# Threshold attention and a SoLU feed-forward: in batch 0, turned weights that stay in place but for corner blocks, and 1/sum multiplied in behind v

## The chip, the cores and the metric

The kernel runs on one core of a Trainium2 chip. Its time is the device time of one launch, in microseconds (us). A profile is one further execution recorded by the hardware profiler. The core has five engines that run their own instruction lists in order and wait for one another by semaphores: TensorE (PE; its weight loads are listed as PEld), VectorE (DVE), ScalarE (ACT), GpSimd (POOL) and SyncE (SP), which here only issues DMAs.

## What is computed

All data are float32 but for the two weight matrices, which are given as float64.

```python
# q, k, v: (8 batches, 8 heads, 576, 64); tau: a number
scores = q @ k.T / sqrt(64)
scores = where(scores >= max(scores, -1) - tau, scores, -1e9)
attn = exp(scores - max(scores, -1))
attn = attn / (sum(attn, -1) + 1e-9)
x = heads_side_by_side(attn @ v)                 # (4608, 512)
h = x @ w_in                                     # (4608, 1024)
solu = h * softmax(h)
ln = (solu - mean) / sqrt(var + 1e-6) * g_ln
out = ln @ w_out                                 # (4608, 512)
```

## The kernel before

**Slots and rounds.** A slot is the scores of 128 query rows against 576 keys for two heads. A batch has 18 slots (`PER`): for each kind (0 and 1) and each of four head pairs two slots (r = 0 and 1), and two slots of kind 2 for the last 64 query rows of all heads. Two slots that follow one another (r = 0, 1) are a unit: they are multiplied with v together. The main loop (line 855) goes through 144 slots and some rounds more; round `rnd` does the scores of slot `rnd`, the second half of slot `rnd - 1`, the product with v of an older unit, and a quarter of a feed-forward tile. Everything lies under `tc.manual_schedule()`: each engine executes its instructions in the order in which the loop writes them.

**One slot.** TensorE writes the scores of both heads to PSUM (`scores`, L434). VectorE goes over them twice, once a head (`maxes`, L455), for row minimum (the scores have a negative sign) and threshold. ScalarE makes the ramp (`ramp`, L470) and the exponentials with their row sums (`exps`, L479) into the tiles `w`. One round later GpSimd makes 1/(sum + 1e-9) (`normalise`, L486 and L487) and multiplies both `w` by it (L489). VectorE then turns `w` in blocks of 32 x 32 (`blocks`, L501) into the tile `T`. When the second slot of a unit is turned, SP's queue moves the whole of `T` to the tile `wT` (L510, L512, for kind 2 L517), which brings the keys onto the partitions of v: one transfer of 576 KB and two of 288 KB, or four of 288 KB. Some rounds later (`pv_due`, line 751: three rounds behind the second slot, four for some) TensorE multiplies v by `wT` in 72 matmuls a unit (`attend_steps`, L542) into a PSUM room, and ScalarE copies that room to the feed-forward's input (`attended`, L572).

**PSUM rooms.** Two rooms `p0` and `p1` serve the product with v, the feed-forward, and in rounds 0, 2 and 4 the turning of q and k of batch 0 (`whole_pair`, L371), which ScalarE copies to SBUF (`keep`, L388 and L390).

**Order inside a round.** In program order: `scores`, `maxes`, `ramp`, `exps`; `whole_pair` in three early rounds; `normalise` of the slot before; jobs of the list `middle` (the feed-forward's statistics, L650); `weight_c`; the feed-forward's step on TensorE (L605 or L710) and the product with v; `attended`; `blocks` of the slot before; jobs of the list `late` (the feed-forward's maximum L620, its multiply L635, its turn L697); and then the weights.

**Weights.** Both weight matrices come as float64 and are put together as float32 from their two 32-bit words, sixteen pieces of 128 x 512, about one a round in rounds 0 to 14. `weight_load` (L251) brings a piece, ScalarE prepares the low word (`weight_e`, L263), VectorE scales the high word by 2^-112 (`weight_m`, L282), masks and shifts it (L286) and sets the sign (`weight_b`, L308), and GpSimd adds the low part one round later (`weight_c`, L332). For the second matrix ScalarE multiplies the gains in (`weight_f`, L340).

**Feed-forward tiles.** The first tile of 128 tokens starts in round 11 (L605, two rounds a tile), its second product (L710) in rounds 17 and 18.

## Time and profile before

| | us |
|---|---|
| runs of the kernel | 857.89, 856.11, 856.63; median 856.63 |
| span of the profiled execution | 854.9 |
| median above that span | 1.7 |

The time of the profiled execution itself isn't listed apart from its span. In rows of groups the columns are line, engine, operation, what is written from what, shapes and count, then busy us, mean ns of one, and the idle time of the engine before them with what ended it. In rows in order of time they are start us, length us, engine, line, operation, and in brackets idle time with its releaser; "x2" is two instructions put together. In rows by stretch they are the stretch, its length, busy us and number of instructions of TensorE, its weight loads, VectorE, ScalarE and GpSimd, then TensorE's granted clock, the DMA share and GB/s. TensorE's busy time counts matmuls that overlap one another, so it isn't a measure of its peak.

### The profile page before, as it was taken

To read this page: it belongs to the slowest core of one execution; us is meant where nothing else is said; L and a number is where in the kernel's file an instruction comes from. 1 tells how busy PE (TensorE), PEld (TensorE's weight loads), DVE (VectorE), ACT (ScalarE), POOL (GpSimd) and SP (SyncE) were. 2 spreads that over 40 slices of the span, in tenths; PEclk is the share of its full clock that TensorE was granted. 3 is DMA by queue.
4 is the path that set the end of the run, shared out by engine and by line. 5 is a ranking of instruction groups with operands and counts; after the bars stand their busy time and mean duration, and the time that the engine had idled before them with its cause. 6 is when DMAs were issued, how large, how long until landed. Compare 5 with 4: busy or idle time off the path is not lost.

```text
span 854.9 us, 36109 instructions
## 1 busy us (share of the span) xinstructions
PE 819.9 (96%) x15363; PEld 620.5 (73%) x15363; DVE 674.6 (79%) x1225; ACT 570.0 (67%) x1127; POOL 496.1 (58%) x945
## 2 busy tenths in 40 slices
PE   6778899999999999999999999999999999999997
PEld 5555677778677787777688877777777777777655
DVE  5997787989788888888788878888888878787361
ACT  6886876777767666667666666666677777775121
POOL 4885656666566656565566666565666655555120
PEclk8899999999999999999999999999999999999999
DMA  9999778798888888887888778887788887655212
GB/s 343 254 249 213 191 194 233 188 259 204 226 229 202 211 185 218 216 216 190 201 215 218 195 177 209 207 217 207 195 221 226 207 188 175 165 137 140 67 38 63
DMA packets 75314, 168.54 MB, mean 197 GB/s; under 512 B 11146, under 2 KB 32658, under 8 KB 75154
## 3 DMA queue, kind: packets, MB, share of 16 engines
q1 hardware_dynamic: 74866, 165.82, 76.7%
q8 instruction: 120, 1.97, 1.0%
q10 hardware_dynamic: 288, 0.43, 0.2%
q14 instruction: 40, 0.33, 0.1%
HBM read 46.14 MB, written 9.44 MB: 65 GB/s over the span
## 4 chain that ended last, share of the span: by engine, by line
PE 83%; DMA 4%; DVE 4%; ACT 3%; issue 2%; POOL 2%; SPq 1%; DVEq 0%; ACTq 0%; POOLq 0%
PE o_ps L710 27%; PE h_ps L605 22%; PE s_ps L434 15%; PE pv L542 14%; DMA wT<-T 3%; PE h_ps L595 3%; ACT w L470 1%; DVE w L455 1%; ACT w L479 1%; DVE T L501 1%; POOL w L489 1%; POOL sm L487 0%; PE s_ps L379 0%; DVE w L308 0%; PE tp L371 0%
## 5 line engine op out<-in xcount | busy, mean ns | idle before, releaser
L710 PE MATMUL o_ps<-w,uT 64*64 64x256 f32 x4608 | 269.5, 376 | 2.2 <-issue 1.6
L470 ACT ACTIVATE w<-s_ps,nth 128x576 f32<-128x576 f32 x280 | 196.8, 738 | 105.6 <-DVE nth L455 88.6
L455 DVE CUSTOM_DVE_ANT_0 w<-s_ps,tau_t 128x576 f32<-128x576 f32 x280 | 200.0, 751 | 83.5 <-PE s_ps L434 52.4
L710 PEld LDWEIGHTS o_ps<-w,uT 64*64 64x64 f32 x4608 | 221.8, 133 | 55.4 <-ACT xh L572 12.0
L489 POOL TENSOR_SCALAR w<-w,sm 128x576 f32<-128x576 f32 x288 | 220.6, 778 | 14.3
L501 DVE STREAM_TRANSPOSE T<-w 128x576 f32<-128x576 f32 x288 | 207.7, 756 | 22.6 <-POOL w L489 22.3
L605 PE MATMUL h_ps<-w,xh 64*64 64x512 f32 x1856 | 220.8, 589 | 0.0
L479 ACT ACTIVATE w<-w,ntau 128x576 f32<-128x576 f32 x288 | 219.6, 767 | 0.0
L542 PEld LDWEIGHTS pv<-wT,v 64*64 64x64 f32 x5760 | 172.6, 136 | 39.8 <-issue 16.7
L434 PE MATMUL s_ps<-kT,qT 64*64 64x512 f32 (+1 forms) x2048 | 175.8, 416 | 13.4 <-ACT w L470 11.3
L542 PE MATMUL pv<-wT,v 64*64 64x128 f32 (+1 forms) x5760 | 173.9, 263 | 8.3 <-DMA wT<-T 7.4
L605 PEld LDWEIGHTS h_ps<-w,xh 64*64 64x64 f32 x1856 | 118.4, 133 | 77.2 <-issue 43.6
L486 POOL TENSOR_SCALAR sm<-sm 128x2 f32<-128x2 f32 x144 | 34.2, 237 | 186.5 <-ACT w L479 182.8
L487 POOL TENSOR_TENSOR sm<-sm,mone 128x2 f32<-128x2 f32 x144 | 106.7, 741 | 12.0
L434 PEld LDWEIGHTS s_ps<-kT,qT 64*64 64x64 f32 x2048 | 72.7, 137 | 21.7 <-ACT w L470 16.2
L572 ACT COPY xh<-pv 128x256 f32<-128x256 f32 x64 | 25.4, 396 | 80.9 <-PE pv L542 80.9
L671 ACT ACTIVATE V<-u,nb,rs 128x1024 f32<-128x1024 f32 x36 | 44.7, 1240 | 40.5 <-POOL nb L661 33.6
L697 DVE STREAM_TRANSPOSE uT<-V 128x1024 f32<-128x1024 f32 x36 | 44.1, 1225 | 15.9 <-DMA V<-u 15.6
L479 ACT ACTIVATION_READ_ACCUMULATOR w<-w,ntau 128x1 f32 x288 | 55.4, 192 | 0.0
L676 DVE TENSOR_SCALAR u<-u,rs,nb 128x1024 f32<-128x1024 f32 x36 | 34.9, 971 | 19.5 <-ACT V L671 17.9
L635 DVE TENSOR_TENSOR u<-h_ps,u 128x1024 f32<-128x1024 f32 x36 | 42.8, 1190 | 9.4 <-ACT u L629 9.4
L620 DVE TENSOR_REDUCE hm<-h_ps 128x1 f32<-128x1024 f32 x36 | 42.9, 1193 | 4.9 <-PE h_ps L595 2.7
(77 smaller groups left out, 553.5 us busy)
## 6 DMA issues: line engine op xcount, KB each, us to landing
wT<-T SPq DMA_DIRECT2D x160, 288.0 KB, 6.5
wT<-T SPq DMA_DIRECT2D x64, 576.0 KB, 5.5
v<-in_v_dram SPq DMA_DIRECT2D x16, 576.0 KB, 6.0
V<-u SPq DMA_DIRECT2D x144, 64.0 KB, 3.5
out_dram<-ob SPq DMA_DIRECT2D x71, 128.0 KB, 2.6
q<-in_q_dram SPq DMA_DIRECT2D x28, 288.0 KB, 6.1
k<-in_k_dram SPq DMA_DIRECT2D x27, 288.0 KB, 6.4
qT<-flip SPq DMA_DIRECT2D x48, 144.0 KB, 3.2
```

What stands on the lines that cost most here:

```text
L434: nc.tensor.matmul(out=ps[h][ROWS[y], ks], lhsT=lhsT, rhs=d["kT"][ROWS[h], ks], start=True, stop=True,)
L455: nc.vector.tensor_tensor_reduce(out=w, in0=ps[:, 0:S], in1=(zero if loose else tau_t).to_broadcast([P, S]), scale=1.0, scalar=BIG, op0=AL ...
L470: nc.scalar.activation(out=d["w"][x], in_=d["w"][x] if d["loose"] else d["ps"][x][:, 0:S], func=AF.Prelu, bias=d["nth"][x], scale=-1.0, al ...
L479: nc.scalar.activation(out=w, in_=w, func=AF.Exp, bias=ntau, scale=1.0, accum_out=sm[:, x : x + 1])
L487: nc.gpsimd.tensor_tensor(out=sm, in0=sm, in1=mone, op=ALU.pow)
L489: nc.gpsimd.tensor_scalar(out=w, in0=w, scalar1=sm[:, x : x + 1], scalar2=1.0, op0=ALU.mult, op1=ALU.mult)
L501: nc.vector.transpose(out=T[:, :, r, h, :], in_=w)
L542: nc.tensor.matmul(out=to, lhsT=d["v"][ROWS[u], (h0 + h - u) % 4, m,], rhs=rhs, start=m == 0, stop=m == NK - 1,)
L605: mm = nc.tensor.matmul(out=h[ROWS[y], f], lhsT=x[ROWS[r], c, ROWS[y]], rhs=w1_parts[ROWS[r], c, part ^ r], start=part == 0 and c == 0, st ...
L671: nc.scalar.activation(out=V, in_=u, func=AF.Identity, bias=nb, scale=rs)
L697: nc.vector.transpose(out=uT, in_=d["V"].rearrange("p y (m x) -> p m y x", x=32))
L710: nc.tensor.matmul(out=d["o"][ROWS[z], 512 * (r ^ other) : 512 * (r ^ other) + 256], lhsT=d["uT"][ROWS[r], m].rearrange("p y x -> p (y x)" ...
```

## The change

It concerns batch 0 alone (slots 0 to 17), but for the shared helper functions.

- `keep` stores the turned k of batch 0 without reordering its columns, so that keys come in chunks of 64.
- `normalise` makes 1/sum as before and no longer multiplies `w`. The sums live in six buffers.
- `corners` takes the place of `blocks`. VectorE turns `w` into `T`, now in an order in which half of the blocks already lie on the partitions where the product needs them. GpSimd copies each turned slot to a second tile `more`; after the second slot four DMAs bring the corner blocks from `more` back into `T` (4 x 32 partitions, 147 KB each). The product reads `T` itself. `corners` returns the copy as a function, which the loop calls behind `weight_b`.
- `spread` is new: behind the product, eight small matmuls by the identity write 1/sum into the same PSUM room, and ScalarE copies it to SBUF. In `attended` two VectorE multiplies take the place of ScalarE's copy for batch 0.
- `weight_s` is new: GpSimd does the scaling by 2^-112 for pieces 4 to 10, two rounds ahead; `weight_m` skips L282 for these.
- `pv_due`: units of slots 1, 3, 5 and 11 come one round earlier.
- `ff_o`: the two output halves of batch 0 are no longer swapped for the second tile.

```diff
@@ weight_m
+            of = d.get("scaled", m)
+            if of is m:
+                nc.vector.tensor_scalar(
+                    out=m.bitcast(F32), in0=hi.bitcast(F32), scalar1=2.0**-112, scalar2=None,
+                    op0=ALU.mult,
+                )
             nc.vector.tensor_scalar(
-                out=m.bitcast(F32), in0=hi.bitcast(F32), scalar1=2.0**-112, scalar2=None,
-                op0=ALU.mult,
-            )
-            nc.vector.tensor_scalar(
-                out=m, in0=m, scalar1=0x7FFFFFFF, scalar2=3,
+                out=m, in0=of, scalar1=0x7FFFFFFF, scalar2=3,
...
+    def weight_s(x):
+        if in_bits(x):
+            hi = raws[x]["raw"].bitcast(F32).rearrange("p (n two) -> p n two", two=2)[:, :, 1]
+            dst = piece(x)[1]
+            nc.gpsimd.tensor_scalar(
+                out=dst, in0=hi, scalar1=2.0**-112, scalar2=1.0, op0=ALU.mult, op1=ALU.mult
+            )
+            raws[x]["scaled"] = dst.bitcast(I32)
@@ keep
         if nm == "k":
+            if i < NP:
+                of, to = room[:, 0 : 64 * len(ms)], pair(i)["kT"][:, 64 * ms[0] : 64 * ms[-1] + 64]
@@ exps
-        d["sm"] = sm = small.tile([P, 2], F32, tag="sm", name="sm")
+        d["sm"] = sm = small.tile(
+            [P, 2], F32, tag="late" if s < PER else "sm", bufs=6 if s < PER else 3, name="sm"
+        )
@@ normalise
         nc.gpsimd.tensor_tensor(out=sm, in0=sm, in1=mone, op=ALU.pow)
+        if s < PER:
+            return
...
+    def corners(s):
+        b, kind, hp, r = slots[s]
+        key = (b, kind, hp)
+        if r == 0:
+            units[key] = dict(
+                T=work.tile([P, NB, 2, 2, 32], F32, tag="T", name="T"),
+                more=work.tile([P, NB, 2, 2, 32], F32, tag="wT", bufs=2, name="wT"),
+                rc=[],
+            )
+        u = units[key]
+        d = live.pop(s)
+        u["rc"].append(d["sm"])
+        T, more = [u[x].rearrange("p (c m) r h x -> p c m r h x", c=2) for x in ("T", "more")]
+        for h, w in enumerate(d["w"]):
+            nc.vector.transpose(out=T[:, :, :, r, h], in_=w.rearrange("p (m c x) -> p c m x", m=NK, c=2))
+
+        def copy():
+            of, to = [u[x][:, :, r].rearrange("p k h x -> p k (h x)") for x in ("T", "more")]
+            nc.gpsimd.tensor_copy(out=to, in_=of)
+            if r == 0:
+                return
+            of, to = [x.rearrange("p c m r h x -> p c (m r h x)") for x in (more, T)]
+            for g in range(2):
+                for half in range(2):
+                    at, src = 64 * half + 32 * (1 - g), 64 * half + 32 * g
+                    nc.sync.dma_start(out=to[at : at + 32, g], in_=of[src : src + 32, 1 - g])
+            u["wT"] = T.rearrange("p g m r h x -> p g m r h x")
+
+        return copy
...
+    def spread(key):
+        b, kind, hp = key
+        unit = units[key]
+        y = unit["y"][1].rearrange("p (u n) -> p u n", u=2)[:, :, 256:384]
+        for r, rc in enumerate(unit["rc"]):
+            for u in range(2):
+                for h in range(2):
...
+                    nc.tensor.matmul(
+                        out=to, lhsT=rc[ROWS[u], h : h + 1].to_broadcast([64, 64]),
+                        rhs=ident[ROWS[u], ROWS[u]].rearrange("p (g x) -> p g x", g=2), start=True, stop=True,
+                    )
+        unit["by"] = by = unit["more"].rearrange("p k r h x -> p (k r h x)")[:, 0:256].rearrange(
+            "p (u n) -> p u n", u=2
+        )
+        nc.scalar.copy(out=by, in_=y)
@@ attended
+        if b == 0:
+            spread(key)
+            by = units[key]["by"]
...
-        nc.scalar.copy(out=to, in_=y)
+        if b == 0:
+            for u in range(2):
+                nc.vector.tensor_tensor(out=to[:, u], in0=y[:, u], in1=view(by)[:, u], op=ALU.mult)
+        else:
+            nc.scalar.copy(out=to, in_=y)
@@ ff_o
-        other = len(t) == 3 and t[2]
+        other = len(t) == 3 and t[0] > 0 and t[2]
@@ the plan
+    LATE = (PER - 1, PER + 9)
+    SCALED = range(4, 11)
...
-            pv_due.append((s + LAG_PV + (s < 6 or s in (11, PER - 1, PER + 9)), (b, kind, hp)))
+            pv_due.append((s + LAG_PV + (s in LATE), (b, kind, hp)))
@@ the loop, behind the product with v
-            if rnd - 1 in live:
+            copied = None
+            if rnd - 1 in live and rnd - 1 < PER:
+                copied = corners(rnd - 1)
+            elif rnd - 1 in live:
                 blocks(rnd - 1)
...
                 weight_b(x)
+                if copied is not None:
+                    copied()
+                    copied = None
...
                     weight_m(x + 1)
+                if x + 2 in SCALED:
+                    weight_s(x + 2)
+            if copied is not None:
+                copied()
```

More of the change, by code (lines that the diff above doesn't have):

```diff
@@ L550, in attend_steps @@
                         yield
+    def spread(key):
[5 more added lines that the diff above has]
+                for h in range(2):
+                    to = y[ROWS[h], u]
+                    if kind == 2:
+                        to = to.rearrange("p (r g x) -> p r g x", r=2, g=2)[:, r]
+                    else:
+                        to = to.rearrange("p (g r x) -> p r g x", r=2, g=2)[:, r]
+                    nc.tensor.matmul(
[6 more added lines that the diff above has]
+        nc.scalar.copy(out=by, in_=y)
     def attended(key):
         b, kind, hp = key
+        if b == 0:
+            spread(key)
+            by = units[key]["by"]
         tag, y = units.pop(key)["y"]
@@ L556, in attended @@
         if kind == 2:
-            y = y.rearrange("p u (r y) -> p u r y", r=2)
+            view = lambda y: y.rearrange("p u (r y) -> p u r y", r=2)
         else:
-            y = y.rearrange("p u (g r x) -> p u g r x", g=2, r=2)
+            view = lambda y: y.rearrange("p u (g r x) -> p u g r x", g=2, r=2)
+        y = view(y)
         if kind == 2:
@@ L571, in attended @@
             to = xh[b, kind][:, hp].rearrange("p (u g x r) -> p u g r x", u=2, r=2, g=2)
-        nc.scalar.copy(out=to, in_=y)
+        if b == 0:
+            for u in range(2):
+                nc.vector.tensor_tensor(out=to[:, u], in0=y[:, u], in1=view(by)[:, u], op=ALU.mult)
+        else:
+            nc.scalar.copy(out=to, in_=y)
         pairs_free.append(tag)
```

## The prediction

> **What bounds the kernel now.** I read first the page's span and busy table, then the busy times by stage, then by round in the first 135 us (a round is one slot of scores, two heads wide; it is cut here at the start of VectorE's pass over its scores), and then the engines' instructions in order of time inside single rounds.
>
> ```profile
> span 854.9 us, 36109 instructions
> PE 819.9 (96%) x15363; PEld 620.5 (73%) x15363; DVE 674.6 (79%) x1225; ACT 570.0 (67%) x1127; POOL 496.1 (58%) x945
> ```
> ```profile
> 0.00:75.00 75.00, 53.28 (x891) 37.89 (x895) 62.04 (x125) 55.98 (x111) 54.40 (x84) 0.88 0.96 273
> 75.00:130.00 55.00, 50.65 (x1115) 38.04 (x1108) 41.69 (x80) 41.63 (x87) 30.73 (x56) 0.95 0.81 195
> 130.00:200.00 70.00, 67.90 (x1255) 52.45 (x1258) 58.47 (x111) 50.07 (x100) 43.71 (x85) 1.00 0.85 219
> 200.00:800.00 600.00, 597.81 (x11349) 460.45 (x11345) 492.89 (x888) 411.10 (x814) 360.22 (x700) 1.00 0.80 199
> ```
>
> The columns are stretch, length, busy us of TensorE, its weight loads, VectorE, ScalarE and GpSimd, granted clock, DMA share, GB/s. From 200 to 800 us TensorE idles 2.2 of 600 us: there the end is set by its work, which this change leaves alone but for 72 small matmuls in batch 0. From 0 to 75 us it idles 21.7. So the change, which lies in batch 0 (rounds 0 to 21, some 130 us), acts by one thing: how late TensorE enters the part that it bounds. A microsecond lost or won there is passed to the end.
>
> ```profile
> 28.64:33.41 4.77, 3.98 (x99) 3.10 (x98) 4.70 (x10) 3.91 (x8) 4.07 (x6) 0.88 0.89 265
> 37.78:42.92 5.14, 3.14 (x34) 2.17 (x38) 4.68 (x10) 4.03 (x8) 4.75 (x7) 0.72 0.98 300
> 47.31:52.16 4.85, 2.85 (x37) 1.82 (x41) 4.69 (x11) 4.23 (x9) 4.25 (x6) 0.81 1.00 277
> 56.54:61.98 5.44, 3.55 (x92) 3.04 (x96) 4.79 (x11) 4.60 (x11) 5.17 (x7) 1.00 0.93 271
> 66.38:78.37 11.99, 8.70 (x126) 6.25 (x122) 6.47 (x11) 4.66 (x9) 7.80 (x11) 0.86 1.04 223
> 83.96:89.52 5.56, 5.56 (x116) 3.99 (x112) 4.73 (x11) 3.74 (x8) 4.41 (x9) 1.00 0.54 134
> 89.52:97.45 7.93, 5.39 (x124) 4.32 (x119) 4.02 (x7) 6.66 (x14) 5.93 (x9) 0.82 0.72 172
> 97.45:102.41 4.96, 3.91 (x94) 2.81 (x90) 4.96 (x9) 3.88 (x9) 1.78 (x4) 0.94 0.84 207
> 113.55:117.24 3.69, 3.37 (x116) 2.96 (x112) 3.65 (x8) 1.95 (x3) 0.94 (x2) 1.00 0.84 211
> ```
>
> These are rounds 4, 6, 8, 10, 12, 14, 15, 16 and 19. In rounds 4 to 10 VectorE (third busy time) is the full one: 4.70 of 4.77, 4.69 of 4.85. Round 12 is the exception, 11.99 us, and the chain of waits says why:
>
> ```profile
> 61.22 12.33 DMA wT<-T
> 73.59 3.27 PE pv L542 x65
> ```
>
> A transfer of turned weights takes 12.33 us at a DMA share of 1.04, and the product with v begins only at 73.59. That is what the change relieves. Now one round of VectorE and of ScalarE, round 7:
>
> ```profile
> 42.92 0.75 DVE L455 CUSTOM_DVE_ANT_0 w<-s_ps,tau_t 128x576 f32<-128x576 f32 x1
> 44.28 1.43 DVE L501 STREAM_TRANSPOSE T<-w 128x576 f32<-128x576 f32 x2
> 45.64 0.83 DVE L308 SCALAR_TENSOR_TENSOR w<-raw,em 128x512 int32<-128x512 int32 x1
> 46.51 0.43 DVE L282 TENSOR_SCALAR em<-raw 128x512 f32<-128x512 f32 x1
> 46.97 0.43 DVE L286 TENSOR_SCALAR em<-em 128x512 int32<-128x512 int32 x1
> 47.31 0.75 DVE L455 CUSTOM_DVE_ANT_0 w<-s_ps,tau_t 128x576 f32<-128x576 f32 x1
> ```
> ```profile
> 43.78 1.42 ACT L470 ACTIVATE w<-s_ps,nth 128x576 f32<-128x576 f32 x2 [1.64 <-DVE nth L455]
> 45.85 0.77 ACT L479 ACTIVATE w<-w,ntau 128x576 f32<-128x576 f32 x1
> 46.62 0.38 ACT L572 COPY xh<-pv 128x256 f32<-128x256 f32 x1
> ```
>
> VectorE goes from its maxes (42.92, two of them) at 44.28 straight into the transposes of the round before, and never asks for anything of this round again. The copy out of the product with v sits on ScalarE at 46.62, behind ramp and exponentials of the same round. It is late there, and nobody on VectorE cares.
>
> **The change, part by part.**
>
> **1. The multiply behind v.** The copy at L572 becomes a chain: 8 small matmuls spread 1/sum, ScalarE copies them to SBUF, and VectorE multiplies twice. In program order these two multiplies stand behind VectorE's maxes and ahead of its transposes, and the ScalarE copy stands behind the exponentials of the same round. So in each round with a product, VectorE, done with its maxes, waits for ramp, exponentials and copy. From round 7: with m the start of the maxes (42.92), the copy begins at m+3.70 and ends at m+4.08 (47.00), while the maxes end at m+1.36. That wait, 2.7 us, is new, and VectorE has nothing else it may do. Queued behind it are transposes, L308, L286 and the next maxes, and for these wait ScalarE and then the next scores.
>
> ```profile
> L635 DVE TENSOR_TENSOR u<-h_ps,u 128x1024 f32<-128x1024 f32 x36 | 42.8, 1190 | 9.4 <-ACT u L629 9.4
> L489 POOL TENSOR_SCALAR w<-w,sm 128x576 f32<-128x576 f32 x288 | 220.6, 778 | 14.3
> ```
>
> Multiply: the same operation over 1024 columns takes 1190 ns; 128 columns by proportion 150, and I take 0.2 each, 0.4 a pair (bounds 0.3 and 0.8). A round with a product is then m+4.2 for the copy and its signal, 0.4 multiply, 1.4 transposes, 0.75 L308, 0.43 L286: 7.2 us. Without the wait it was 4.39 (42.92 to 47.31).
>
> **2. VectorE loses L282** for weight pieces 4 to 10: 7 x 0.43 = 3.0 us, all in rounds 2 to 8. I count it in the 7.2. In rounds without a product it is worth less, since there the chain max, ramp, scores takes over:
>
> ```profile
> 33.12 2.29 PE L542 MATMUL pv<-wT,v 64*64 64x128 f32 x72 [0.79 <-ACT qT L390]
> 40.11 2.18 PE L434 MATMUL s_ps<-kT,qT 64*64 64x64 f32 x12 [0.35 <-ACT w L470]
> 45.25 1.19 PE L434 MATMUL s_ps<-kT,qT 64*64 64x64 f32 x12 [0.34 <-ACT w L470]
> ```
>
> Twelve score matmuls take 2.18 us behind an idle TensorE and 1.19 behind a product. From m to the end of the ramps is 2.3 (45.20 - 42.92), plus 2.2: 4.5 us, against 4.4 to 4.6 before. Nothing won there.
>
> **3. GpSimd** loses two passes (2 x 0.78) a round and gains one copy of 1152 columns, not in the trace as such: at the rate of L489 1.5 us; from below a third of it, from above twice. It also gets the scaling of pieces 4 to 10, some 0.8 us by the same rate. Round 8 has it 4.25 us busy; 5.1 fits beside an average of (7.2 + 4.5)/2 = 5.9. Hidden; not hidden above a copy of about 2.3 us. That the transposes no longer wait for GpSimd's normalising is worth at most the few tenths that VectorE idles in round 8 (4.85 - 4.69).
>
> **4. DMA.**
>
> ```profile
> wT<-T SPq DMA_DIRECT2D x160, 288.0 KB, 6.5
> ```
>
> Two such transfers and one of twice the size are a unit of kind 0 or 1 now, with a median of 6.5 us to landing. A unit moves 0.59 MB in place of 1.18, four transfers for three on SP's queue, the same order of issue time. With about 6 units within the first 75 us it is 3.5 MB less of 20.5 (273 GB/s x 75 us). The product's wait for data in round 12 goes.
>
> **5. Products earlier.** Units of slots 1, 3 and 5 go to rounds 4, 6 and 8, that of slot 11 from round 15 to 14. Round 4 also turns the last pair through the same PSUM rooms, which ScalarE empties late:
>
> ```profile
> 30.08 1.50 DVE L501 STREAM_TRANSPOSE T<-w 128x576 f32<-128x576 f32 x2
> 32.34 0.72 ACT L390 ACTIVATE qT<-tp,scl 128x576 f32<-128x576 f32 x1
> ```
>
> The product can start at 33.1 (in the trace above it did, one round later, waiting for just this), ends at 35.4, spread 35.8, copy 36.3, multiplies 36.85, transposes 38.3, L308 39.0, L286 39.45. The next maxes were at 33.41 and are at 39.45: 6.0 us lost.
>
> **6. Spread matmuls**: 72 in all, by the product's 72 in 2.29 us some 3 us for the batch, from below nothing where TensorE idles; inside the waits above. The k copy without reordering is taken at nothing (same elements), the swapped output rooms too.
>
> **Round 12, the gain, and round 16.**
>
> ```profile
> 101.74 0.39 ACT L572 COPY xh<-pv 128x256 f32<-128x256 f32 x1
> ```
> ```profile
> 66.06 3.80 PE L605 MATMUL h_ps<-w,xh 64*64 64x512 f32 x32
> 69.91 1.22 DVE L620 TENSOR_REDUCE hm<-h_ps 128x1 f32<-128x1024 f32 x1 [0.29 <-PE h_ps L605]
> ```
>
> The first row is the copy of round 16, 4.3 us behind the start of its maxes. In round 12 before, VectorE did transposes, L620, L308 and the next piece during the 12 us. Now all of it queues behind the multiply. From m: scores end m-0.4, h m+3.5, product m+6.5, spread and copy m+7.3, multiply m+7.8, transposes m+9.2, L620 m+10.4, L308 m+11.1, L282 and L286 m+12.0. So the data come early and the round still takes 12.0. **The relief is real and is eaten by the queue.**
>
> **The sum** (new length less old): round 4 +6.0; rounds 6 and 8 (7.2) +2.1 and +2.35; round 10 (7.65, L282 back) +2.2; rounds 5, 7, 9, 11 together +0.8 (4.55 to 4.6 each); round 12 0; round 14, which now has h and product (copy at m+6.3, then 2.6 us) +3.3; round 15 without its product -1.6; round 16 (exponentials end m+4.3, then copy, multiply and the 3.5 us that follow the maxes: 9.0) +4.0; rounds 17 and 18 -1; round 19 +2.5; rounds 20 to 22 +0.5. That makes +21; about 1 of it is lateness of VectorE that TensorE, by then the bound, doesn't feel. I take **+20**. On the profiled execution 854.9 becomes about 875; the runs' median, 856.63, lies 1.7 above its span, and I keep that: **876.6 us**.
>
> **Rivals.**
>
> **A. VectorE and GpSimd block one another (slower still).** GpSimd's copy starts when the transposes end, with L308 and L286 next on VectorE.
>
> ```profile
> 50.26 1.05 DVE L308 SCALAR_TENSOR_TENSOR w<-raw,em 128x512 int32<-128x512 int32 x1
> 64.69 0.74 DVE L308 SCALAR_TENSOR_TENSOR w<-raw,em 128x512 int32<-128x512 int32 x1
> 71.77 0.86 DVE L282 TENSOR_SCALAR em<-raw 128x512 f32<-128x512 f32 x1
> ```
>
> Beside GpSimd passes L308 took 1.05 in place of 0.74, and L282 0.86 in place of 0.43: some 0.3 to 0.4 each, not a whole pass. If one of them waited out the whole 1.5 us copy, 12 rounds bound by VectorE lose 1 us more each: about 889. The Trainium skill's page "SBUF — State Buffer", section "SBUF: two separate sides", says that the pair of ports these engines share is an exclusive lock for a whole instruction; by that rule this rival is the forecast, and the delays above speak for only part of it. Chance 0.10.
>
> **B. The DMA relief wins (faster).** Place: round 12 and the waits for wT. Price: up to 7.4 us in round 12 (11.99 against some 4.6), 0.8 in round 10, and up to 3 for L282: 856.6 - 11 = about 846. It decides if in rounds with a product the transposes still start within 0.3 us of the maxes, that is, if the multiply doesn't hold the queue or its operands are ready by then. For it speaks the DMA share of 0.96 over 75 us. Against it: the copy's earliest start, m+3.7, follows from VectorE's own maxes of that round, so no relief elsewhere can bring it forward. Chance 0.10.
>
> **C. Half of the waits are covered.** Rounds with a product keep VectorE waiting, but the lost time of round 4 and of rounds 14 to 21 is taken back where ScalarE or TensorE led anyway (round 15 takes 7.93 us with VectorE 4.02 busy). Then only rounds 6, 8, 10 and some 3 us of the others are left: about +9, 866. Chance 0.13. That nothing changes, the relief just paying for the waits, has 0.03.
>
> **How the numbers follow.** Forecast 0.64 (its own range 869 to 884: multiply 0.3 to 0.8 and its signals, 9 units, -2 to +4; GpSimd's copy and scaling 0 to +5; rounds 14 to 22 by +-4), A 0.10, B 0.10, C 0.13, no change 0.03. The range 861 to 889 takes in the forecast, C, and A to its value, and leaves out B, no change and the tails. About 0.2% is what a measurement of this kernel can tell from no change. Faster 0.10, same 0.03, slower 0.87.
>
> **What the profile after would show.** Right: in rounds 4, 6, 8, 10, 12, 14, 16, 19 and 21 VectorE idles some 2.7 us or more, released by the ScalarE copy, and its multiply comes next, then the transposes; product waits for wT gone; the DMA share of the first 75 us well below 0.96; round 4 near 10.8 us. Wrong would be transposes right behind the maxes in these rounds, a round 12 near 5 us, or GpSimd's copy at 3 us and more, which would make GpSimd the bound.

## The result, and the profile after

The changed kernel took 883.13 us in the median of four runs (891.66, 879.65, 883.17, 883.1), beside 857.26 for the kernel before (856.11 to 858.07, four runs): a ratio of 1.0327, 95% interval 1.0272 to 1.0383. It is 26 us slower. The forecast was 876.6 with a range of 861 to 889. The profiled execution of the changed kernel is the slowest of its four, 891.66 us with a span of 889.4; the spans of the others are 877.4 to 880.9. So single rounds are read from that trace below, and the whole from medians.

Span and busy times, then busy times by stage (columns as before):

```profile
span 889.4 us, 36426 instructions
...
PE 837.1 (94%) x15507; PEld 622.0 (70%) x15507; DVE 679.5 (76%) x1236; ACT 570.8 (64%) x1127; POOL 499.0 (56%) x934
```
```profile
0.00:75.00 75.00, 48.24 (x835) 36.53 (x839) 50.31 (x100) 47.71 (x96) 44.23 (x62) 0.80 0.65 208
75.00:130.00 55.00, 44.64 (x764) 30.78 (x760) 40.19 (x80) 34.77 (x72) 29.40 (x42) 0.88 0.52 128
130.00:200.00 70.00, 65.09 (x1316) 50.40 (x1308) 51.79 (x103) 45.93 (x93) 39.13 (x76) 0.95 0.69 179
200.00:800.00 600.00, 594.63 (x11342) 449.06 (x11346) 493.89 (x892) 414.54 (x822) 364.01 (x704) 1.00 0.82 202
```

In the first 75 us the DMA share fell from 0.96 to 0.65, as it should. But VectorE is busy 50.3 us there in place of 62.0, TensorE 48.2 in place of 53.3 with its granted clock at 0.80 in place of 0.88: each engine idles more. From 200 to 800 TensorE is nearly as full as before (594.6 of 600 us in place of 597.8). Most of the loss lies in front of it. Rounds 4, 6, 8, 10, 12, 14, 15, 16, 19 and 21, cut at the start of the maxes as in the prediction:

```profile
28.79:41.41 12.62, 7.56 (x170) 6.54 (x166) 4.95 (x11) 5.04 (x10) 4.48 (x6) 0.83 0.19 73
46.09:53.72 7.63, 3.51 (x99) 2.63 (x94) 4.95 (x12) 3.75 (x8) 4.50 (x6) 0.95 0.53 181
58.40:66.02 7.62, 4.13 (x98) 3.25 (x92) 4.94 (x12) 4.36 (x9) 4.41 (x6) 0.86 0.27 104
71.04:79.20 8.16, 7.92 (x126) 5.77 (x118) 5.45 (x12) 4.39 (x9) 4.09 (x6) 0.81 0.50 148
84.23:94.66 10.43, 10.12 (x168) 5.55 (x160) 5.80 (x14) 4.75 (x10) 4.45 (x6) 0.99 0.48 127
100.04:109.11 9.07, 8.25 (x192) 5.98 (x184) 5.17 (x14) 5.87 (x11) 3.46 (x8) 0.92 0.24 62
109.11:115.23 6.12, 3.54 (x52) 2.69 (x56) 3.51 (x8) 4.66 (x11) 5.78 (x7) 0.71 0.51 119
115.23:124.00 8.77, 5.89 (x123) 4.90 (x118) 5.44 (x11) 3.87 (x9) 1.98 (x4) 0.81 0.58 144
134.48:141.59 7.11, 6.95 (x160) 4.84 (x152) 4.50 (x10) 3.21 (x7) 3.72 (x7) 1.00 0.59 134
146.20:157.50 11.30, 9.36 (x214) 6.47 (x210) 4.79 (x11) 4.10 (x9) 4.93 (x9) 0.80 0.84 212
```

Round 6 went from 5.14 to 7.63 with VectorE 4.95 busy (4.68 before). The waits between 20 and 160 us (engine, line, for whom, us in total, times, longest) name the idle time:

```profile
POOL wT L528 <- DVE T L524: 34.3, 10, 8.0
...
DVE xh L646 <- ACT wT L618: 29.7, 8, 7.6
...
DVE xe L646 <- ACT wT L618: 6.1, 1, 6.1
```

VectorE's multiply behind v (L646) waits 35.8 us in nine units for ScalarE's copy of the spread sums (L618, into a part of the tile that holds the copied slots). No row of these waits has the product waiting for a transfer any more; before, it waited for `wT` in round 12. One such round in order of time, round 6, on VectorE, on ScalarE and on GpSimd:

```profile
50.10 0.49 DVE L646 TENSOR_TENSOR xh<-pv,wT 128x128 f32<-128x128 f32 x2 [2.58 <-ACT wT L618]
50.51 1.43 DVE L524 STREAM_TRANSPOSE T<-w 128x576 f32<-128x576 f32 x2
51.86 0.65 DVE L319 SCALAR_TENSOR_TENSOR w<-raw,em 128x512 int32<-128x512 int32 x1
52.62 1.18 DVE L288 TENSOR_SCALAR em<-w 128x512 int32<-128x512 int32 x1
```
```profile
49.72 0.35 ACT L618 COPY wT<-pv 128x256 f32<-128x256 f32 x1
```
```profile
52.00 1.52 POOL L528 COPY wT<-T 128x1152 f32<-128x1152 f32 x1 [2.96 <-DVE T L524]
```

The maxes ended at 47.5. Then VectorE stands for 2.58 us, until ScalarE's copy has ended, and all its work of the round queues behind the multiply. There is a second thing: the mask (L288) takes 1.18 us where it took 0.43 (L286), and it ends at 53.80, just behind the end of GpSimd's copy (53.52). The groups show it for all of batch 0 (line, count, then busy us and mean ns):

```profile
L319 DVE SCALAR_TENSOR_TENSOR w<-raw,em 128x512 int32<-128x512 int32 x16 | 10.9, 683 | 0.1
L288 DVE TENSOR_SCALAR em<-w 128x512 int32<-128x512 int32 x7 | 8.3, 1181 | 0.7
L284 DVE TENSOR_SCALAR em<-raw 128x512 f32<-128x512 f32 x9 | 7.2, 796 | 5.5 <-DMA raw<-in_moe_w_in_dram 5.3
```
```profile
L528 POOL COPY wT<-T 128x1152 f32<-128x1152 f32 x18 | 25.2, 1400 | 36.2 <-DVE T L524 34.9 <-ACT w L483 0.8 <-issue 0.5
L302 POOL TENSOR_SCALAR w<-raw 128x512 f32<-128x512 f32 x7 | 5.7, 817 | 0.0
```

### The profile page after: what moved, and what is told of

It reads as the page before. It is cut to its first block, busy times and chain, and to the rows that moved or that the text cites. A ratio compares the mean times of both kernels' runs of the same rounds, so it can differ in the third digit from the quotient of the medians.

```text
span 889.4 us, 36426 instructions
## 1 busy us (share of the span) xinstructions
PE 837.1 (94%) x15507; PEld 622.0 (70%) x15507; DVE 679.5 (76%) x1236; ACT 570.8 (64%) x1127; POOL 499.0 (56%) x934
## 4 chain that ended last, share of the span: by engine, by line
PE 74%; DVE 7%; DMA 4%; issue 4%; ACT 3%; SPq 2%; POOL 2%; DVEq 0%; ACTq 0%; POOLq 0%
PE o_ps L786 24%; PE h_ps L681 20%; PE s_ps L447 14%; PE pv L589 13%; DMA wT<-T 4%; PE h_ps L671 3%; DVE w L468 2%; ACT w L483 1%; DVE T L524 1%; SPq L763 1%; DVE T L548 1%; DVE bs L726 1%; ACT w L494 1%; POOL w L506 1%; POOL sm L502 0%
## 5 line engine op out<-in xcount | busy, mean ns | idle before, releaser
L681 PE MATMUL h_ps<-w,xh 64*64 64x512 f32 x1856 | 224.6, 601 | 0.2 <-DVE xh L646 0.2
L447 PE MATMUL s_ps<-kT,qT 64*64 64x64 f32 (+1 forms) x2048 | 177.1, 424 | 26.7 <-ACT w L483 23.7
L506 POOL TENSOR_SCALAR w<-w,sm 128x576 f32<-128x576 f32 x252 | 195.1, 786 | 12.5
L548 DVE STREAM_TRANSPOSE T<-w 128x576 f32<-128x576 f32 x252 | 181.5, 755 | 20.8 <-POOL w L506 20.8
L681 PEld LDWEIGHTS h_ps<-w,xh 64*64 64x64 f32 x1856 | 115.8, 136 | 86.8 <-issue 54.2
L589 PEld LDWEIGHTS pv<-wT,v 64*64 64x64 f32 x5040 | 146.0, 133 | 30.7 <-issue 18.4
L589 PE MATMUL pv<-wT,v 64*64 64x128 f32 (+1 forms) x5040 | 147.3, 259 | 3.7 <-issue 2.8
L447 PEld LDWEIGHTS s_ps<-kT,qT 64*64 64x64 f32 x2048 | 70.3, 138 | 36.1 <-ACT w L483 30.2
L648 ACT COPY xh<-pv 128x256 f32<-128x256 f32 x56 | 22.4, 401 | 74.5 <-PE pv L589 74.5
L705 ACT ACTIVATE u<-h_ps,hm 128x1024 f32<-128x1024 f32 x36 | 40.1, 1114 | 20.1 <-DVE hm L696 15.1
```

Source lines behind the costliest of these rows:

```text
L447: nc.tensor.matmul(out=ps[h][ROWS[y], ks], lhsT=lhsT, rhs=d["kT"][ROWS[h], ks], start=True, stop=True,)
L506: nc.gpsimd.tensor_scalar(out=w, in0=w, scalar1=sm[:, x : x + 1], scalar2=1.0, op0=ALU.mult, op1=ALU.mult)
L548: nc.vector.transpose(out=T[:, :, r, h, :], in_=w)
L589: nc.tensor.matmul(out=to, lhsT=d["v"][ROWS[u], (h0 + h - u) % 4, m,], rhs=rhs, start=m == 0, stop=m == NK - 1,)
L681: mm = nc.tensor.matmul(out=h[ROWS[y], f], lhsT=x[ROWS[r], c, ROWS[y]], rhs=w1_parts[ROWS[r], c, part ^ r], start=part == 0 and c == 0, st ...
```

## The experiments

Twelve kernels. The lateness of a kernel is the time at which VectorE begins the maxes of a round, less that in the kernel before, one profile each:

| us late at round | 12 | 14 | 20 | 23 | 143 |
|---|---|---|---|---|---|
| the change | +17.9 | +16.1 | +24.4 | +27.9 | +33.8 |
| mult_late | +6.7 | +1.0 | +4.2 | +9.8 | +9.3 |
| best_b | +4.0 | -1.6 | +2.8 | +4.7 | +3.5 |
| no_mult | +5.2 | -0.8 | -0.9 | +1.5 | +10.1 |
| no_mult_b | +3.7 | -2.3 | -0.3 | -2.7 | -0.9 |
| scaled_alone | +1.9 | -4.5 | -5.5 | -2.1 | -1.4 |
| copy_alone | +3.2 | -2.9 | -3.4 | -2.8 | -0.9 |
| no_transfer_b | -0.1 | -6.7 | -6.7 | -5.9 | -4.4 |

**mult_late: the same multiplies, at the end of VectorE's round.** Each pair is issued behind the transposes and the weights of its round.

```diff
+        def multiply():
             for u in range(2):
                 nc.vector.tensor_tensor(out=to[:, u], in0=y[:, u], in1=view(by)[:, u], op=ALU.mult)
+            pairs_free.append(tag)
+        return multiply
...
             if copied is not None:
                 copied()
+            if multiply is not None:
+                multiply()
```

> The changed kernel with one edit: batch 0's two multiplies are issued at the end of the round on VectorE, behind the transposes and the weight work, in place of ahead of the transposes. Theory Q (the multiply holds VectorE's queue): the 35.8 us that VectorE waits for ScalarE's copy ahead of the multiplies in the changed kernel go nearly all; VectorE's work in these rounds fills the time of ramp and exponentials; some 20 us come back, 858 to 866 us. Theory L (GpSimd's copy locks VectorE out, its masks of 1.18 us in place of 0.43, and that is most of the loss): at most 6 us come back, 876 us and more. In both the maxes of round 4 to those of round 5 tell: about 5 us by Q, 11 or more by L.

Measured: 866.78 (865.04 to 867.89), ratio 1.0121 (1.0086 to 1.0156). VectorE in its round 6:

```profile
44.15 1.43 DVE L524 STREAM_TRANSPOSE T<-w 128x576 f32<-128x576 f32 x2
45.51 0.79 DVE L319 SCALAR_TENSOR_TENSOR w<-raw,em 128x512 int32<-128x512 int32 x1
46.41 1.18 DVE L288 TENSOR_SCALAR em<-w 128x512 int32<-128x512 int32 x1
47.50 0.47 DVE L651 TENSOR_TENSOR xh<-pv,wT 128x128 f32<-128x128 f32 x2
```

The transposes follow the maxes at once, and the multiply no longer waits. Its rounds 6 and 12 by stretch:

```profile
42.80:47.90 5.10, 3.63 (x102) 2.75 (x94) 5.00 (x11) 3.76 (x8) 4.94 (x6) 0.91 0.02 6
...
73.03:78.81 5.78, 5.04 (x124) 3.41 (x116) 5.71 (x13) 4.60 (x10) 4.85 (x7) 1.00 0.94 240
```

They take 5.10 and 5.78 us in place of 7.63 and 10.43. That gives back 16 us: the place in the queue is the larger part of the loss. The time lies just above the 858 to 866 that were expected, and one sign named there didn't come: round 4 takes 9.50 us, neither about 5 nor 11. The product still waits there for the room of the last pair, and VectorE stands 4.31 us at the multiply, now behind its other work.

**no_mult: spread, copy and multiplies left out**, ScalarE's copy of the product in their place.

```diff
-        if b == 0:
-            spread(key)
-            by = units[key]["by"]
...
-            for u in range(2):
-                nc.vector.tensor_tensor(out=to[:, u], in0=y[:, u], in1=view(by)[:, u], op=ALU.mult)
-        else:
-            nc.scalar.copy(out=to, in_=y)
+        nc.scalar.copy(out=to, in_=y)
```

> The changed kernel with spread matmuls, copy to SBUF and multiplies left out: ScalarE copies the product as before, so batch 0's outputs lack the factor 1/sum. Corners, GpSimd copy, scaling and earlier products stay. Theory Q: the same as with the multiplies late, within 3 us, 856 to 864 us; what is left against before is GpSimd's copy against VectorE, some 0.7 us a round. Theory L: 874 us and more.

Measured: 865.58 (861.7 to 869.79), ratio 1.0111 (1.0074 to 1.0148), not to be told from mult_late (four and six runs). So in this pair the chain at the end of the round has no price that can be told; best_b and no_mult_b below, twelve runs each, do give it one. What is left, some 9 us, is elsewhere, and by the table not all in batch 0: in its trace this kernel is 0.9 us ahead of the kernel before at round 20, 1.5 behind at round 23 and 10.1 at the last slot. From round 23 to the last slot TensorE idles 7.5 us in it, 3.1 before, above all in two stalls of 2.2 and 2.0 us for which the profile names no releaser. Nothing in the change was shown to make them.

**old_lag: the change with the products in their old rounds.**

```diff
-    LATE = (PER - 1, PER + 9)
+    LATE = (1, 3, 5, 11, PER - 1, PER + 9)
```

> The changed kernel with the products of the units of slots 1, 3, 5 and 11 in the rounds of before (5, 7, 9 and 15). Theory Q: round 4 falls from 12.6 us to about 5 and rounds 5, 7 and 9 take the 3.3 us wait in place of 4, 6 and 8, so 4 to 6 us come back: 877 to 879 us. If the turning of the last pair in round 4 is not what makes its wait long, nothing comes back: 883 us.

Measured: 877.28 (874.62 to 882.59), ratio 1.0256 (1.0198 to 1.0314). Its rounds 4 and 5:

```profile
27.85:32.53 4.68, 4.64 (x92) 3.76 (x93) 4.16 (x9) 3.90 (x8) 4.52 (x6) 0.68 0.52 198
32.53:40.15 7.62, 3.44 (x104) 2.42 (x97) 4.94 (x12) 4.53 (x10) 4.47 (x6) 1.00 0.87 249
```

Without a product round 4 takes 4.68 in place of 12.62, and the product of round 5 costs 7.62 like any other: some 6 us of the loss (5.9 by the medians of four runs each) are the price of the earlier products, round 4 above all. There, in the changed kernel, TensorE, ScalarE and VectorE show:

```profile
33.19 3.88 PE L589 MATMUL pv<-T,v 64*64 64x128 f32 x72 [1.93 <-ACT qT L403]
```
```profile
37.39 0.37 ACT L618 COPY wT<-pv 128x256 f32<-128x256 f32 x1 [3.72 <-issue]
```
```profile
37.80 0.49 DVE L646 TENSOR_TENSOR xh<-pv,wT 128x128 f32<-128x128 f32 x2 [7.57 <-ACT wT L618]
```

The product waits for the room of the last pair until 33.19, as the prediction had it, and then takes 3.88, where the prediction used 2.29; VectorE stands for 7.57 us. The two products by stretch, the changed kernel's first, then the one before:

```profile
33.19:37.07 3.88, 3.88 (x86) 3.88 (x90) 0.00 (x0) 0.48 (x1) 0.00 (x0) 0.56 0.00 0
```
```profile
33.12:35.41 2.29, 2.29 (x74) 2.06 (x74) 2.29 (x6) 1.87 (x4) 2.19 (x4) 1.00 1.00 235
```

TensorE's granted clock was 0.56 over the first and 1.00 over the second. Up to 800 us the trace grants TensorE half its clock for 54.6 us in the changed kernel, 34.1 in mult_late and 23.9 in the kernel before, in stretches of 3.4 or 6.8 us; each of them, in these three kernels, begins directly behind 3.4 us in which TensorE stood for 1.5 us or more. So in these traces a wait that leaves TensorE standing is often followed by slower matmuls. How much of the 26 us this makes wasn't measured apart.

**no_transfer: the kernel before without any transfer of turned weights in batch 0.** The product reads `T` itself, so the keys of batch 0 lie in the wrong rows.

```diff
-            units[key] = dict(T=work.tile([P, NB, 2, 2, 32], F32, tag="T", name="T"))
+            units[key] = dict(T=work.tile([P, NB, 2, 2, 32], F32, tag="wT" if b == 0 and s // 2 % 2 else "T", bufs=2, name="T"))
...
+        if b == 0:
+            u["wT"] = T.rearrange("p (g m) r h x -> p g m r h x", g=2)
+            return
```

> The kernel before, with batch 0's product reading the turned tile itself, so that none of its turned weights are moved (keys are then in the wrong rows, the output of batch 0 is not the reference's); the tiles take four buffers. Nothing of the multiply. Theory Q, which holds the relief of the transfers for real: round 12 falls from 12.0 us to 7 or 8, rounds 10 and 11 by up to 1, the rest stays, 850 to 853 us. If the queue of transfers is not what holds round 12, 857 us.

Measured: 855.17 (850.6 to 858.95), ratio 0.9991 (0.9966 to 1.0016), between the two expectations. Round 12 took 5.57 us in place of 11.99, and the kernel was 7.7 us ahead at round 20, but round 21 took 10.52 in place of 6.09:

```profile
123.17 1.44 DVE L501 STREAM_TRANSPOSE T<-w 128x576 f32<-128x576 f32 x2 [6.24 <-DMA wT<-T]
```

The turned tile of the last unit of batch 0 is now held until its product in round 21. By its releaser the wait is for transfers of the unit between, issued 114.13 to 119.02: the first slot turned in round 21 seems to have got that unit's tile, still being read. mult_late has the same row (6.87 us at 134.74), and in the changed kernel the wait is hidden behind the multiply of round 21.

**no_transfer_b: the same with the two buffer tags exchanged** (`s // 2 % 2 == 0`), so that another tile comes round.

> The kernel before with no transfer of batch 0's turned weights, as in no_transfer, with the buffers so arranged that the transposes of round 21 don't need the tile that the product of the same round reads (keys in the wrong rows, output not the reference's). no_transfer was 7.7 us ahead of the kernel before up to round 20 and lost 4.4 in round 21. If holding the tile was why, the lead stays: 848 to 851 us. If the lead goes later all the same (TensorE waits elsewhere), 854 to 856 us.

Measured: 850.92 (848.82 to 854.29), ratio 0.9942 (0.9913 to 0.9971). Rounds 12 and 21:

```profile
66.25:71.84 5.59, 5.59 (x120) 3.33 (x116) 5.42 (x12) 4.18 (x9) 5.14 (x8) 1.00 0.92 240
116.11:122.21 6.10, 6.10 (x196) 4.72 (x190) 4.38 (x10) 4.29 (x9) 3.50 (x7) 1.00 0.96 255
```

Both waits are gone, and all that remains is 0.6%, some 5 us. It is the most that the relief of the DMA queues alone gave, with every transfer gone and nothing put in its place. The lead of 6.7 us shrinks to 4.4 by the last slot.

**late_three and best_a: three buffers for the turned tiles.** late_three is mult_late with three buffers for `T` and one for `more`; best_a also puts the products of slots 1, 3 and 5 back by a round.

```diff
-                T=work.tile([P, NB, 2, 2, 32], F32, tag="T", name="T"),
-                more=work.tile([P, NB, 2, 2, 32], F32, tag="wT", bufs=2, name="wT"),
+                T=work.tile([P, NB, 2, 2, 32], F32, tag="abc"[s // 2 % 3], bufs=1, name="T"),
+                more=work.tile([P, NB, 2, 2, 32], F32, tag="d", bufs=1, name="wT"),
...
-        unit["by"] = by = unit["more"].rearrange("p k r h x -> p (k r h x)")[:, 0:256].rearrange(
+        unit["by"] = by = unit["T"].rearrange("p k r h x -> p (k r h x)")[:, 0:256].rearrange(
```

> The kernel with the multiplies late (866.8 us), and the turned tiles of batch 0 in three buffers with one for the copy, in place of two and two, the spread sums put into the turned tile. In all runs that read the turned tile in place, round 21 takes 9.3 to 11.6 us in place of 6.1: VectorE's transposes of slot 20 need the tile that the product of round 21 still reads. If that holding costs, round 21 falls to about 6 us and the time by 3 to 5 us: 862 to 864 us. If round 21 is long for another reason, 866 to 867 us.

> As the run before (late multiplies, three buffers), and the products of the units of slots 1, 3 and 5 one round later again, as in the kernel before. Round 4 should fall from 9.5 to about 4.7 us, for the product of round 4 waits there for a PSUM room and the scores of round 5 stand behind it on TensorE. Theory Q with the transfers' relief (6 us in round 12): 4 to 5 us less than the run before, 857 to 860 us. If the relief is as large as round 12 shows and nothing else is left, below the kernel before, 850 to 855 us. If early products are worth something, no change against the run before.

Measured: 864.6 (860.08 to 867.28), ratio 1.0093 (1.0062 to 1.0123); and 865.12 (864.88 to 866.42), ratio 1.0105 (1.0062 to 1.0148), which is no gain over late_three. In late_three the transposes of round 21 no longer wait, but the round takes 9.59 us and not the 6 expected: there TensorE stands for 2.46 us among the scores that follow the spread matmuls, and the profile names no releaser. mult_late, the changed kernel and best_b have that stall too (1.93, 1.94 and 1.94 us), no_mult and no_mult_b, which have no spread matmuls, don't. In best_b it is this row:

```profile
134.21 1.19 PE L447 MATMUL s_ps<-kT,qT 64*64 64x64 f32 x10 [1.94 <-issue]
```

So the held tile is one part of what round 21 lost. Round 4 of best_a is 4.71, but a wait has taken the place of the ones removed:

```profile
POOL wT L528 <- DMA T<-wT: 14.3, 7, 3.5
```

With one buffer for the copies GpSimd waits until the corner transfers of the unit before have read it. Rounds 9 to 13 together take 33.0 us in best_a and 27.4 in mult_late.

**copy_act: the changed kernel with the slot's copy on ScalarE** (`nc.scalar.copy` for `nc.gpsimd.tensor_copy` at L528).

> The changed kernel (883.1 us) with the copy of the turned slot on ScalarE in place of GpSimd. Theory L in its smaller form (while GpSimd copies, VectorE's mask at 1.18 us in place of 0.43 waits for the end of the copy): the mask falls to 0.43, rounds with a product from 7.6 to 6.9 us, and 5 to 8 us come back, 875 to 878 us. If VectorE is not locked out by the copy: 883 us, or more by ScalarE's added 1.2 us a round.

Measured: 889.68 (888.13 to 890.27), ratio 1.0386 (1.0341 to 1.043): slower still. The number is that of the second expectation, but not for the reason given there. In its round 6 ScalarE, VectorE and GpSimd show:

```profile
44.25 1.15 ACT L528 COPY wT<-T 128x1152 f32<-128x1152 f32 x1
45.30 1.37 ACT L483 ACTIVATE w<-s_ps,nth 128x576 f32<-128x576 f32 x2
```
```profile
50.97 1.52 DVE L288 TENSOR_SCALAR em<-w 128x512 int32<-128x512 int32 x1
```
```profile
50.95 1.26 POOL L343 TENSOR_TENSOR w<-w,em 128x512 int32<-128x512 int32 x1 [1.68 <-DVE w L319]
```

The copy now stands ahead of the ramp, on which everything in the round waits. And the mask is 1.52 us long, not 0.43: without the copy GpSimd goes on to its next pass (L343, the low words) as soon as the sign is set, at 50.95, that is, beside the mask, which ends at 52.49, 0.28 us behind it. So another GpSimd pass in this place holds the mask as well, and this kernel doesn't isolate the copy.

**best_b and no_mult_b: two of the remaining waits taken out.** best_b is mult_late with the products of slots 1, 3 and 5 a round later and the buffers of `T` and `more` exchanged for kind 2; no_mult_b makes the same two edits to no_mult. So the two differ by the chain alone: spread matmuls, copy and multiplies.

```diff
-    LATE = (PER - 1, PER + 9)
+    LATE = (1, 3, 5, PER - 1, PER + 9)
...
-                T=work.tile([P, NB, 2, 2, 32], F32, tag="T", name="T"),
-                more=work.tile([P, NB, 2, 2, 32], F32, tag="wT", bufs=2, name="wT"),
+                T=work.tile([P, NB, 2, 2, 32], F32, tag="wT" if kind == 2 else "T", name="T"),
+                more=work.tile([P, NB, 2, 2, 32], F32, tag="T" if kind == 2 else "wT", bufs=2, name="wT"),
```

> The changed kernel with three edits: multiplies at the end of the round, products of the units of slots 1, 3 and 5 in rounds 5, 7 and 9, and for the unit of kind 2 the turned tile and its copy exchanged between the two pairs of buffers, so that round 21 need not wait. Two buffers each as in the changed kernel. If the single buffer for the copy was what best_a lost in rounds 9 to 13 (8 us more than the kernel with late multiplies and two buffers), the whole is 5 us below the runs of 865: 857 to 860 us. If late products themselves cost there, 863 to 866 us.

> As best_b, but with spread, copy to SBUF and multiplies left out (batch 0 lacks the factor 1/sum) and ScalarE copying the product as before. What is left against the kernel before is corners, GpSimd's copy against VectorE's passes, GpSimd's scaling, and the relief of the transfers (7 us at round 20, 4 at the end, as no_transfer_b measured). Theory Q with its four terms (multiply's queue, product in round 4, tile held in round 21, GpSimd's copy): the first three are gone, so 851 to 856 us. If there is a further cost not named, 860 us and more.

Measured: 862.12 (859.37 to 865.2), ratio 1.0069 (1.0043 to 1.0096), the best version of the change, and still slower than before; and 858.57 (856.02 to 866.12), ratio 1.002 (0.9988 to 1.0052), level with it. Both lie between their two expectations. The medians differ by 3.6 us, the means of twelve runs by 3.5 with a 95% interval of about 1.3 to 5.7: even at the end of the round the chain has a price. Round 21 alone is 3.0 us longer with it (9.64 us, 6.64 in no_mult_b). In no_mult_b round 7 still takes 6.15 in place of 4.39, and TensorE and VectorE say why:

```profile
42.37 3.46 PE L589 MATMUL pv<-T,v 64*64 64x128 f32 x72
```
```profile
45.94 1.44 DVE L524 STREAM_TRANSPOSE T<-w 128x576 f32<-128x576 f32 x2 [1.50 <-ACT w L483]
```

The transposes begin when the product ends (45.83): with the product a round later, it still reads the tile that the new unit is to be turned into. The view names ScalarE, whose work was long done. With `T` held until its product, the product costs a wait in either place: for the PSUM room when early, for the tile when late.

**scaled_alone: the kernel before with `weight_s`,** the scaling of pieces 4 to 10 on GpSimd, and nothing else of the change.

> The kernel before with one part of the change: GpSimd scales weight pieces 4 to 10 and VectorE skips that pass. Prediction's step 2: 3.0 us of VectorE gone, worth little where max, ramp and scores bound the round: 0 to -2 us, 854 to 856. If the added GpSimd pass of 0.8 us delays the normalising that VectorE's transposes wait for, or locks its masks out: +1 to +4 us.

Measured: 858.69 (853.18 to 863.71), ratio 1.002 (0.9987 to 1.0052): no difference that can be measured. Its profile holds a warning: round 12 takes 5.58 us, with every transfer still in place.

```profile
68.26:73.84 5.58, 5.58 (x118) 4.27 (x114) 5.41 (x12) 3.87 (x9) 5.14 (x8) 1.00 1.03 261
```

It is 5.5 us ahead at round 20, and at the last slot 1.4. So round 12's 12 us may have belonged partly to how transfers happened to meet in one execution. And the early lead isn't all kept: in round 22 TensorE stands for 3.46 us with no releaser named (1.59 before).

**copy_alone: no_transfer_b with GpSimd's copy in place of its two passes.** In batch 0 GpSimd doesn't multiply `w` by 1/sum; it copies each turned slot in place, behind `weight_b`.

```diff
+        if s < PER:
+            return
         for x, w in enumerate(d["w"]):
...
+            at = T[:, :, r].rearrange("p k h x -> p k (h x)")
+            return lambda: nc.gpsimd.tensor_copy(out=at, in_=at)
```

> The kernel without transfers in batch 0 (850.92), in which GpSimd's two multiplies of the exponentials by 1/sum are also left out in batch 0 (so batch 0 lacks 1/sum, and its keys lie in wrong rows as before) and GpSimd copies each turned slot in place instead, behind the sign of the weights, as in the changed kernel. No small transfers, no multiplies behind v, old rounds of the products, VectorE keeps its scaling of the weights. Theory: GpSimd's copy holds up VectorE's weight passes, scaling and masks (1.2 us in place of 0.43 in rounds 2 to 13), by some 0.7 us a round where VectorE is the full engine: 853 to 857. Rival: the copy costs nothing (3 us of GpSimd's work for 2 passes less), and what the kernel without multiply and with exchanged buffers (858.57) has lost comes from products that hold the turned tile: 849.5 to 852.

Measured: 855.99 (852.05 to 859.12), ratio 0.9992 (0.9966 to 1.0017), beside 0.9942 (0.9913 to 0.9971) without the copy: some 4 to 5 us for a copy that is shorter than the passes it replaces. Round 7, VectorE and GpSimd:

```profile
47.11 0.65 DVE L308 SCALAR_TENSOR_TENSOR w<-raw,em 128x512 int32<-128x512 int32 x1
47.80 1.25 DVE L282 TENSOR_SCALAR em<-raw 128x512 f32<-128x512 f32 x1
```
```profile
47.32 1.45 POOL L507 COPY T<-T 128x1152 f32<-128x1152 f32 x1 [1.01 <-DVE T L503]
```

The scaling begins beside the copy and ends at 49.05, 0.28 us behind the copy's end at 48.77, with 1.25 in place of 0.43. The sign pass (L308) also lies beside the copy and is not longer, but it began first, and there it is the copy that is longer: the 12 copies that begin 0.09 to 0.21 us behind a sign pass take 1.45 to 1.59 us, the other six 1.14 or 1.15. Where a sign pass begins second it is the longer one: the prediction's row of 1.05 us at 50.26 in the kernel before began beside this one.

```profile
49.49 1.28 POOL L332 TENSOR_TENSOR w<-w,third 128x512 int32<-128x512 int32 x1
```

So in these rows whichever pass begins later is held for about as long as the other has left. Each round is 5.03 us in place of 4.4 to 4.86. In the kernel before, GpSimd's passes lay beside the transposes and the sign, and left the scaling and the mask free (0.43 each in round 7). The Trainium skill's page "SBUF — State Buffer", section "SBUF: two separate sides", says that a GpSimd instruction and a VectorE one that uses the shared ports (in a two-port mode, or with two inputs in SBUF) don't share them: the one that starts first has them for its whole instruction, and the other blocks. The scaling (1.25 against 0.43), the copy behind a sign pass (1.45 against 1.15) and the sign pass behind GpSimd's addition (1.05 against 0.65 to 0.69) agree with it; which ports a pass uses no run here shows.

## Why the prediction was right, and where its terms were off

**The ladder.** Medians, each step one thing more: 855.2 to 857.3 before; 850.9 without transfers; 856.0 with GpSimd's copy; 858.6 with the corner transfers, held tiles and the weights' scaling (no_mult_b); 865.6 with the products early and the tile held in round 21 (no_mult); 866.8 with the multiplies at the end of the round (mult_late); 883.1 with the multiplies where the change put them. They were measured at several times, and the runs of one kernel spread over some 2 to 12 us, so a step of 1 to 3 us is not shown; those of 16, 7 and 5 are. But for the 7 (no_mult_b to no_mult) the traces give only 4.2 by round 23; the rest arises in later rounds, which the edit doesn't touch.

**Step 1, the multiply: right, and the main cause.** A wait of 2.7 us per round with a product was forecast, 2.58 measured in round 6; a round of 7.2, measured 7.63 and 7.62, and 8.16 for round 10 (7.65). The mask of 1.18 us, in round 10 the scaling of 1.26, each in place of 0.43, more than covers the excess. Moving nothing but these multiplies gives 16 us back.

**Step 2, L282: right that it is worth little**; alone it can't be measured (1.002, 0.9987 to 1.0052).

**Step 3, GpSimd: the durations were right, the cover was not.** The copy was put at 1.5 us (1.40 in the mean) and the scaling at 0.8 (0.82), and both fit GpSimd's time. But the price is on VectorE: the mask took 1.18 us in place of 0.43, and the scaling, where VectorE still does it, 0.80 in the mean. Rival A named the mechanism with 12 us more than the forecast; copy_alone puts it at 4 to 5. A "hidden" instruction on an engine with room was taken at nothing though it makes another engine's wait. The prediction read its rows of 1.05 and 0.86 us as a loss of 0.3 to 0.4, "not a whole pass"; these passes had begun while a GpSimd pass was running, the first 0.77 us into one of 1.28, and waited for about what was left of it. The change issues the copy right ahead of the next weight pass, so nearly all of it is left.

**Step 4, DMA: right in kind.** The product's waits for `wT` went. All of it is worth about 5 us (no_transfer_b). Rival B's 11 us fell: mult_late, where the queue no longer eats the relief, has a round 12 of 5.78 and is still 1.2% slower than before.

**Step 5, round 4: +6.0 forecast, +7.9 measured** (12.62 less 4.77). The wait for the room was as forecast; the product took 3.88 instead of 2.29, at a granted clock of 0.56, and the mask 1.18.

**Step 6, the spread matmuls:** the forecast counted 72 matmuls as the program writes them, and its row of 2.29 us counts them as the profile does, two for each: the profile has 144 more than before. By that row they make 4.6 us, not some 3. The forecast put them inside the waits; best_b and no_mult_b put the whole chain at 3.6 us.

**Round 12 and the later rounds** (forecast, then measured, new length less old): round 12 0, -1.6; round 14 +3.3, +3.5; round 15 -1.6, -1.8; round 16 +4.0, +3.8; round 19 +2.5, +3.4; rounds 20 to 22 together +0.5, +3.5. The last is the term that was missed: round 21 takes 11.30 in place of 6.09. Its multiply waited 6.1 us, which belongs to step 1; but mult_late and no_transfer show that behind it lies a wait of its own, for a tile that the change holds through the product. The prediction has no term for how long `T` is held, and none for TensorE's stall behind the spread matmuls.

**The sum.** +20 was taken, +25.9 is measured. By its own steps the trace has +28 at round 23, where the prediction's rounds end. Of the other 6 us up to the last slot, 2.9 are added idle time of TensorE (6.0 us in place of 3.1 from round 23 on), above all one stall of 2.4 us near 448 for which the profile names no releaser; 3.4 us at half clock follow it. This is one execution, 8.5 us above its median; nothing in the change was shown to make these losses.

By cause the forecast fits less well than by number. Nearly all of its +20 stood on the multiplies' place in the queue, and moving them away gives back 16. The other 10 us are what is left of round 4, the copy beside VectorE, the held tile and the chain's price at the end of the round, most of which it put at nothing. That these made up the difference is in part luck.

**Rival C** (half of the waits covered, +9) fell: rounds 14, 16 and 19 lost what was forecast for them. Whether the copy of the spread sums could come ahead of ScalarE's exponentials wasn't tried.

## What to carry to other kernels

Before an operation is put on an engine, look at what stands behind it in program order: a pair of multiplies of 0.49 us that waited 2.6 us and more at the head of VectorE's queue cost 16 us in nine places. At the end of the round the whole chain behind v cost 1 to 4 us. A transfer saved is worth what its wait cost on the path that sets the end (here 5 us of 855), and the buffer that is kept in its place is held longer and makes waits of its own. And a pass that fits an idle engine is not free while another engine slows beside it: compare the durations of its neighbours in the same stretch.

## What the hardware showed that was not expected

VectorE's mask and scaling of 0.43 us took 1.18 to 1.26 when begun beside a GpSimd copy that was running, ending some 0.3 us behind it. The order of the starts decides which pass is longer: a sign pass begun 0.09 us or more ahead of the copy took 0.64 to 0.79 us (0.65 to 0.69 with no pass beside it) and the copy 1.45 us or more in place of 1.15, while a sign pass begun beside a running GpSimd pass took up to 1.07.

The 72 matmuls of one product, 2.29 us in the row that the prediction used, took 3.88 in round 4 of the change and 3.46 in round 7 of no_mult_b; the granted clock over these products was 0.56 and 0.64, over the row of 2.29 it was 1.00. A single row was too little for this term.

The runs of the changed kernel spread over 12 us (879.65 to 891.66), the four runs of the kernel before beside them over 2; fifteen runs of it beside mult_late spread over 10 (852.97 to 862.87). The granted clock over the changed kernel's first 75 us was 0.80, that of the kernel before 0.88; whether the clock makes the spread wasn't tested.
